# A gated attention and GLU kernel: where the splits of the row maxima, the casts and the low parts of q and k stand in VectorE's and ScalarE's order

## The chip, the core and the metric

The kernel runs on one core of a Trainium2 chip. The time is the device time of one execution in microseconds. The kernel before took 734.03 us (median of three runs, 732.46 to 734.10).

## The reference, cut to what matters

```python
def _A_ref(x, wqkv, wo):                      # S = 2048, D = 512, H = 32 heads of 16, window W = 256
    qkv = (x @ wqkv).reshape(B, S, 3, H, Dh).transpose(2, 0, 3, 1, 4)
    q, k, v = qkv[0], qkv[1], qkv[2]
    scores = einsum("bhqd,bhkd->bhqk", q, k) * Dh ** -0.5
    mask = (i - j >= 0) & (i - j < W)
    p = softmax(where(mask, scores, -1e9))
    return einsum("bhqk,bhkd->bhqd", p, v).transpose(0, 2, 1, 3).reshape(B, S, D) @ wo

def _B_ref(x, w_gate, w_up, w_down):          # F = 1376
    return (sigmoid(x @ w_gate) * (x @ w_up)) @ w_down

g = sigmoid((x * gate_w).sum(-1, keepdims=True))
return g * _A_ref(x, wqkv, wo) + (1 - g) * _B_ref(x, w_gate, w_up, w_down)
```

All is in fp32. The kernel makes each fp32 product out of three products of high and low parts (`mm3`): a high part is a cast to fp32r on ScalarE (ACT), a low part is the difference on VectorE (DVE).

## The kernel before

The order of the instructions on PE, ACT, DVE and SP (the queue of the DMAs) is the order in which the program writes them (`manual_schedule`). GpSimd (POOL) has only the masks here.

**Units.** The main loop `for u in range(N)` runs over units. A unit is a block of 128 queries in a group of four heads (8 groups of 16 blocks, 128 units). It has four steps, one for each head `hh`; a step is called a *slot* here. In a slot, PE makes the scores `s` (`s_part`, L370), from which DVE takes the row maximum (tile `mx`, L376), and the transposed scores `st` of nine units earlier (`st_part`, L425), of which ACT takes the exponential (L430). The two stand on different halves of the array and run side by side. Scores have two banks in turn (tag `s`, `bufs=2`): the `s` after next waits until DVE has read the maximum of this one.

**Fill.** Between them PE works on projections of q and k (`pj`), the gate and up products (`gu`) and later others, all through `group_mm` (L282), also two at a time on the two halves. `GAPS2` gives how many such pairs follow each slot: three in most, two in the *dense* slots. A *period* is eight units, 31 slots with a gap and one without.

**Bursts.** Every eighth unit (17, 25, ... 121, `visits[u] == 2`) starts with a long burst on PE: the products of probabilities and values for two blocks of 512 queries (`pv_part`, L460), the first into bank `pv`, the second into a bank with tag `st`. ACT copies each out (`o_take`, tile `ob`), and the transfers follow on SP. No slot runs meanwhile.

**Splits of the maxima.** Every fourth unit from 13 on (`mark`) `max_split` makes high and low parts of 16 columns of maxima, with three small DVE instructions (L386, L387, L391, tiles `nm` and `nt`), ahead of that unit's slots; `max_store` and `max_load` send them into the ring of operands. One of two such units is a burst's; the other is in the middle of the period (slot 16 of it).

**Guests.** Other small work is put into two lists, `acts` for ACT and `behind` for DVE, and taken from them in certain slots: the casts and low parts of weights (`w`, `wqh`, `wql`) and those of q and k. A q and k projection of one block is copied out of its bank by `proj_raw` (tile `pr`), cast by `proj_hi` (tile `sh`, L306), and its low part is made by `proj_lo` (tile `sl`, L310). Two of them make a stack, which goes to `stack_scratch` and comes back into the ring by `stack_load` (a fill and five loads, three DMAs a unit). Before, these casts and low parts were guests in the slots of the middle and of the end of a period.

**Masks.** `mask_p` issues one or two `affine_select` on POOL (L436, L442) at a unit's end, when its exponentials are made; so POOL works in the first one and a half slots of the next unit.

Of the kernel before, what the change touches and what calls it, by code (L numbers as in the profile page):

```python
# [39 lines left out]
LAG = 9  # L40
PVLAG = LAG + 4
# [3 lines left out]
QB = 32  # L45
HOLD = 3
GAPS = [3] * 12 + [2] * 3
GAPS2 = [3] * 8 + [2] * 3 + [3] * 6 + [2] * 3 + [3] * 8 + [2] * 3
SHIFT = 6
TURN = ((0, 2, 1), (1, 0, 2))  # L50
TAIL_LOAD = {109: 0, 110: 1, 114: 2, 115: 3}
# [14 lines left out]
def gated_mix_kernel(  # L66
# [53 lines left out]
    NP = NSTEP // 2  # L120
# [23 lines left out]
    with ExitStack() as actx:  # L144
# [466 lines left out]

        def proj_out(s):
            proj_raw(s)
            held.append((s, lambda: (proj_hi(s), behind.insert(0, lambda: proj_lo(s)))))

        halves = {}
        soon = []
# [115 lines left out]
        def flush(acts):  # L733
            while acts:
                acts.pop(0)()
# [89 lines left out]
        sdma = []  # L825
        wo_raw = []

        U_WIDE = NB * NWIDE + LAG
        visits = {u: 2 for u in range(PVLAG + 4, U_WIDE + 1, WIDE)}
        visits.update({u: 1 for u in range(U_WIDE + 4, N, 4)})  # L830

        proj_at = {5: [5], LAG: [6, 7], U_LAST: [NSTEP - 2], U_LAST + 1: [NSTEP - 1]}
        for s in range(8, NSTEP - 2):
            proj_at.setdefault(4 * s - (21 if s % 2 else 17), []).append(s)

        for u in range(N):
            if u == LAG:
                vctx.close()
                pctx = ExitStack()
                ppool = pctx.enter_context(tc.tile_pool(name="ppool", bufs=1))  # L840
                pbuf = ppool.tile([P, 15, HG, P], F32, name="pbuf")
                pv = ps.tile([P, CH], F32, tag="pv", name="pv", bufs=1)
            if u == 1:
                proj_post(NC)
            if u == 4:
                load_gu(0, 0)
                load_gu(0, 1)
            if u % 8 == 1 and u > 8 and u // 8 + 1 < NP:
                sdma = stack_load(u // 8 + 1)
            if u % 16 == 8 and u // 16 + 2 < NG:  # L850
                raw_q = load_wqk(u // 16 + 2)
            if u in (4, 8, NU):
                max_store(u // 4 - 1)
            mark = PVLAG <= u < NU and (u - PVLAG) % 4 == 0

            def transfers():
                if mark and visits.get(u) != 2:
                    run_dmas(later[:2])
                    del later[:2]
                    max_load((u - 5) // 4)  # L860
                run_dmas(later)
                later.clear()
                run_dmas(sdma[:SD])
                del sdma[:SD]

            if u in V_STORE:
                v_store(V_STORE[u])
            if not mark:
                transfers()
            if u in (5, LAG):  # L870
                max_load(u // 4 - 1)
            if u in V_LOAD:
                v_load(V_LOAD[u])
            if u in WD_LOAD:
                load_d(WD_LOAD[u])
            if u == NU:
                max_load(NSTEP - 1)
            if u in TAIL_LOAD:
                tail_load(TAIL_LOAD[u])
            if u == WO:  # L880
                both = apool.tile([P, ND, CH], F32, tag="w0", name="woraw")
                wo_raw.extend(both[:, d] for d in range(ND))
                nc.sync.dma_start(both, wo.rearrange("(c p) n -> p c n", p=P))
            for s4 in proj_at.get(u, ()):
                if u < LAG:
                    first.insert(0, (
                        lambda k, h, s4=s4: proj_slot(s4, k, h), lambda s4=s4: proj_sum(s4)))
                else:
                    work.append(proj_group(s4))
            while held and u >= 8 * (held[0][0] // 2) - 13:  # L890
                acts.append(held.pop(0)[1])
            if u == N - 1:
                hold_group(*rest.pop(0))
            for hh in range(HG):
                wide = visits.get(u) == 2
                if hh == 0 and u in visits:
                    s2 = (u - PVLAG) // 4 - wide
                    pv_part(s2, pv)
                if hh == 0 and mark:
                    max_split((u - 5) // 4)  # L900
                    run_dmas(later)
                    later.clear()
                    max_store((u - 5) // 4)
                if hh == 0 and wide:
                    flush(evac)
                    o_take(s2, pv)
                    run_dmas(later)
                    later.clear()
                    max_load((u - 5) // 4)
                    second = ps.tile([P, CH], F32, tag="st", name=f"pv{s2}", bufs=2)  # L910
                    pv_part(s2 + 1, second)
                    for guests, n in ((acts, 2), (behind, 4)):
                        for _ in range(min(n, len(guests))):
                            guests.pop(0)()
                    o_take(s2 + 1, second)
                elif hh == 0 and u in visits:
                    evac.append(lambda s2=s2: o_take(s2, pv))
                if hh == 2 and mark:
                    transfers()
                if u < NU:  # L920
                    s_part(u, hh)
                if 0 <= u - LAG < NU:
                    st_part(u - LAG, hh ^ 1 if u < NU else hh)
                if u < LAG:
                    flush(behind)
                    if hh % 2 == 1:
                        upto = n_first * (2 * u + 1 + hh // 2) // (2 * LAG)
                        run_first(upto - done)
                        done = upto
                else:  # L930
                    long = u < U_WIDE
                    k8 = (u - LAG) % WIDE * HG + hh
                    dense = GAPS2[max(0, k8 - 1)] < 3 if long else u < NU and (u - PVLAG) % 4 == 3 and hh > 0
                    k = (u - PVLAG) % 4 * HG + hh
                    at = k8 if long else k
                    guests, more = ((1, 3, 6, 12, 14, 21, 23, 26), (5, 25)) if long else ((1, 5, 9), (3, 7))
                    if behind and (u < PVLAG or u >= NU or at in guests or at in more and len(behind) > 2):
                        behind.pop(0)()
                    if evac:
                        evac.pop(0)()  # L940
                    elif acts and not dense and (u < NU or hh % 2 == 1):
                        acts.pop(0)()
                if u >= LAG and (hh % 2 == 1 or u < NU) and (u + 1 not in visits or hh < HG - 1):
                    if u < N - 2:
                        next(slots)
            if u < LAG:
                flush(soon)
            if u == LAG - 1:
                split_gu(0, 0)
                split_gu(0, 1)  # L950
            if u in (3, 7, NU - 1):
                max_split(u // 4)
            if u // 16 + 2 < NG:
                if u % 16 == 10:
                    acts.append(lambda g=u // 16 + 2, r=raw_q: (
                        split_wqk(g, r, 0), behind.insert(0, lambda: split_wqk(g, r, 1))))
            if 0 <= u - LAG < NU:
                mask_p(u - LAG)
            if u in TAIL_SPLIT:
                acts.append(lambda d=TAIL_SPLIT[u]: tail_split(d))  # L960
            if u in WD_SPLIT:
                acts.append(lambda f=WD_SPLIT[u]: split_d(f, True))
            if u in WO_SPLIT:
                acts.extend(lambda d=d: wo_split(d) for d in range(WO_SPLIT[u], WO_SPLIT[u] + 1))
            if u in SUMS:
                sums_load(SUMS[u])
            if u - 2 in SUMS:
                behind.append(lambda c=SUMS[u - 2]: later.append(sums_invert(c)))
            if u == TREAD:
                tail_reads(0)  # L970
            if u >= TREAD:
                tail_read(0, 2)
            for n in H_LOAD.get(u, ()):
                h_load(n)
            if u == N - 1:
                pctx.close()
                lpool = actx.enter_context(tc.tile_pool(name="lpool", bufs=1))
                gates = lpool.tile([P, 4 * NB], F32, name="gates")
                gs, omg = gates[:, 0:NB], gates[:, NB:2 * NB]
                spare = [lpool.tile([P, CH], F32, name=f"spare{k}") for k in range(6)]  # L980
            if u >= N - 2:
                flush(evac)
                flush(acts)
                flush(behind)
                h_skew(u - N - 1)
# [164 lines left out]
```

## Time and profile before

| | |
|---|---|
| median of three runs | 734.03 us (732.46 to 734.10) |
| the profiled execution | 733.71 us, its span 731.7 us |
| PE busy | 720.6 us of the span |
| PE weight loads busy | 591.8 us |
| DVE busy | 485.4 us |
| ACT busy | 427.5 us |
| POOL busy | 167.1 us |
| granted TensorE clock | 1.00 |

The span is what the profiler saw of the program; the execution's own time is 2.0 us more. Matmuls overlap, and their ends are modelled, so the pitch of the starts tells more than the busy time. A row of the timeline has the start in us, the duration in us, the engine, the line, the instruction, and in brackets how long the engine idled before it and what released it.

### The profile page before, as it was taken

What the parts mean: (1) busy time and instruction counts of PE and PEld (TensorE: products, weight loads), DVE (VectorE), ACT (ScalarE), POOL (GpSimd) and SP (SyncE); (2) the same over time, 40 slices, a digit from 0 to 9 for tenths busy, and PEclk for the clock granted to TensorE, in tenths of its full rate; (3) what the DMA queues carried; (4) which work ended last, traced back from release to release, by engine and by line L of the source; (5) the groups of instructions that cost most, each with busy time, mean ns of one, the idle gap of its engine ahead of it and who ended that gap; (6) DMA issues with size and microseconds to landing.
All of it is one profiled execution on the core that took longest, in us unless ns stands there. A gap on an engine that the chain in (4) does not pass through costs nothing.

```text
span 731.7 us, 17525 instructions
## 1 busy us (share of the span) xinstructions
PE 720.6 (98%) x6298; PEld 591.8 (81%) x6298; DVE 485.4 (66%) x1455; ACT 427.5 (58%) x890; POOL 167.1 (23%) x254
## 2 busy tenths in 40 slices
PE   9999999999999999999999999999999999999997
PEld 7888888878787787887878778798878888888886
DVE  5379857657585675867667586675837777658481
ACT  6423766667576676757758666675667664534341
POOL 5200323223242232323223332232332000000000
PEclk9999999999999999999999999999999999999999
DMA  8476644544464445635445445454577987879431
GB/s 297 113 203 201 211 147 182 164 158 169 125 229 155 152 130 170 213 118 198 149 148 181 154 156 181 166 173 131 177 227 196 252 239 184 217 174 252 127 80 57
DMA packets 104814, 127.22 MB, mean 174 GB/s; under 512 B 46718, under 2 KB 63614, under 8 KB 104728
## 3 DMA queue, kind: packets, MB, share of 16 engines
q1 hardware_dynamic: 104584, 125.98, 55.8%
q8 instruction: 49, 0.80, 0.5%
q14 instruction: 37, 0.30, 0.1%
q10 hardware_dynamic: 144, 0.13, 0.1%
HBM read 71.80 MB, written 51.13 MB: 168 GB/s over the span
## 4 chain that ended last, share of the span: by engine, by line
PE 89%; DVE 6%; issue 3%; DMA 1%; SPq 0%; ACT 0%; DVEq 0%
PE gu L282 22%; PE pv L460 11%; PE pj L282 11%; PE s L370 6%; PE tp L598 6%; PE st L425 5%; PE pd L94 5%; PE pd L96 5%; PE pd L95 5%; DVE junk L376 4%; PE vh L635 3%; PE pa L94 2%; PE pa L95 2%; PE pa L96 2%; PE vps L497 2%
## 5 line engine op out<-in xcount | busy, mean ns | idle before, releaser
L376 DVE CUSTOM_DVE_ANT_0 junk<-s,mask 128x384 f32<-128x384 f32 (+2 forms) x512 | 271.6, 530 | 136.0 <-PE s L370 71.9
L282 PE MATMUL gu<-xh,w 64*128 64x512 f32 x1152 | 272.2, 391 | 0.0
L282 PE MATMUL gu<-xl,w 64*128 64x512 f32 x576 | 184.7, 389 | 0.0
L370 PE MATMUL s<-ring 64*128 64x384 f32 (+2 forms) x536 | 167.2, 330 | 5.2 <-DVE mx L376 4.7
L430 ACT ACTIVATE pbuf<-st 128x384 f32<-128x384 f32 (+2 forms) x288 | 138.3, 491 | 57.3 <-PE st L425 31.5
L425 PE MATMUL st<-ring 64*128 64x384 f32 (+2 forms) x536 | 170.0, 334 | 0.9 <-DMA ring<-max_scratch 0.6
L282 PEld LDWEIGHTS gu<-xh,w 64*128 64x128 f32 x1152 | 155.7, 185 | 6.9
L430 ACT ACTIVATE V<-st 128x384 f32<-128x384 f32 (+2 forms) x224 | 101.3, 455 | 54.8 <-PE s L370 27.0
L370 PEld LDWEIGHTS s<-ring 64*128 64x128 f32 x536 | 95.0, 184 | 36.5 <-DVE mx L376 22.9
L436 POOL TENSOR_SCALAR_AFFINE_SELECT pbuf<-pbuf 128x512 f32<-128x512 f32 x72 | 46.8, 650 | 256.4 <-ACT pbuf L430 240.5
L425 PEld LDWEIGHTS st<-ring 64*128 64x128 f32 x536 | 95.5, 184 | 5.2 <-ACT V L430 1.6
L282 PEld LDWEIGHTS gu<-xl,w 64*128 64x128 f32 x576 | 90.8, 184 | 2.7
L282 PE MATMUL pj<-xh,wqh 64*128 64x512 f32 (+1 forms) x228 | 79.8, 391 | 0.0
L282 PE MATMUL pj<-xl,wqh 64*128 64x512 f32 (+1 forms) x228 | 79.5, 389 | 0.0
L282 PE MATMUL pj<-xh,wql 64*128 64x512 f32 (+1 forms) x228 | 69.6, 390 | 0.0
L436 POOL TENSOR_SCALAR_AFFINE_SELECT V<-V 128x512 f32<-128x512 f32 x56 | 36.8, 657 | 116.9 <-ACT V L430 112.2
L95 PE MATMUL pd<-ring,hb 128*128 128x512 f32 x160 | 62.3, 389 | 0.0
L96 PE MATMUL pd<-ring,hb 128*128 128x512 f32 x160 | 62.3, 389 | 0.0
L94 PE MATMUL pd<-ring,hb 128*128 128x512 f32 x160 | 62.3, 389 | 0.0
L90 ACT CAST hb<-V 128x512 fp32r<-128x512 f32 x40 | 24.9, 622 | 58.3 <-DVE V L798 44.8
L471 ACT COPY ob<-pv 128x512 f32<-128x512 f32 x32 | 18.8, 586 | 54.6 <-PE pv L460 51.5
L460 PE MATMUL pv<-pbuf,V 128*32 128x384 f32 (+2 forms) x848 | 49.5, 381 | 0.0
(131 smaller groups left out, 1280.2 us busy)
## 6 DMA issues: line engine op xcount, KB each, us to landing
gu_scratch<-sp SPq DMA_DIRECT2D x72, 256.0 KB
V<-gu_scratch SPq DMA_DIRECT2D x36, 512.0 KB
ring<-stack_scratch SPq DMA_DIRECT2D x56, 256.0 KB
stack_scratch<-sh SPq DMA_DIRECT2D x14, 512.0 KB
stack_scratch<-sl SPq DMA_DIRECT2D x14, 512.0 KB
ring<-stack_scratch SPq DMA_DIRECT2D x14, 512.0 KB
guraw<-in_wgu_dram SPq DMA_DIRECT2D x18, 256.0 KB
v_scratch<-V SPq DMA_DIRECT2D x4, 1088.0 KB
```

Source lines behind the costliest of these rows:

```text
L90: nc.scalar.copy(hi, src)
L94: mm(ps, lh, rh, start=first, stop=False)
L95: mm(ps, lh, rl, start=False, stop=False)
L96: mm(ps, ll, rh, start=False, stop=last)
L282: return mm(pt, (wl if w == 2 else wh)[r, d], (xl if w == 1 else xh)[r, d, c * CH:(c + 1) * CH], start=k == 0 and not second, stop=k == 3 ...
L370: mm(pt[:, (k - k0) * P:(e - k0) * P], lhsT, blk(g, k, hh, 1, e - k), start=k == k0, stop=e == i + 1, skip_group_check=True,)
L376: nc.vector.tensor_tensor_reduce(junk[:, 0:n], pt[:, 0:n], mask[:, 3 * P - n:], scale=1.0, scalar=NEG, op0=ALU.add, op1=ALU.max, accum_out ...
L425: mm(pt[:, (q - j) * P:(e - j) * P], lhsT, blk(g, q, hh, 0, e - q), start=q == j, stop=e == last, skip_group_check=True,)
L430: exps.append(nc.scalar.activation(p_blk(u, hh, 0, n), pt[:, 0:n * P].rearrange("p (b t) -> p b t", t=P), AF.Exp, scale=SCALE,))
L436: nc.gpsimd.affine_select(buf[:, s0], buf[:, s0], pattern=[[0, HG], [1, P]], compare_op=ALU.is_ge, fill=0.0, base=0, channel_multiplier=-1,)
L460: mm(bank[32 * hh:32 * hh + w, (q - q0) * P:(e - q0) * P], vt[:, v:v + w], p_blk(g * NB + j, hh, q - j, e - q), start=j == j0, stop=j == q ...
L598: return mm(tp[b][:, 0:TW], (xl if w == 1 else xh)[r, d, b * P:(b + 1) * P], tw[d][int(w == 2)][r, 0:TW], start=k == 0 and not second, sto ...
```

## The change

It has five parts.

1. `max_split` of a middle unit (`mid(u)`) is written one slot earlier, ahead of the last slot of the unit before.
2. The cast and low part of q and k leave the lists. `held` keeps the copies, and in the burst that comes before their stack is loaded, `proj_hi` of both stands ahead of the first `o_take`, `proj_lo` of both behind the transfers of the maxima; the stack's stores are issued there. Up to three more low parts are taken in the burst, four before.
3. Other low parts are taken in the long periods only at `hh == 2`, and not in the unit ahead of a middle unit.
4. The second group of dense slots goes from slots 17 to 19 to slots 21 to 23.
5. The projections of q and k are queued two units later, and `stack_load` starts one unit later, behind the burst.

```diff
-GAPS2 = [3] * 8 + [2] * 3 + [3] * 6 + [2] * 3 + [3] * 8 + [2] * 3
+GAPS2 = [3] * 8 + [2] * 3 + [3] * 10 + [2] * 3 + [3] * 4 + [2] * 3
...
         def proj_out(s):
             proj_raw(s)
-            held.append((s, lambda: (proj_hi(s), behind.insert(0, lambda: proj_lo(s)))))
+            held.append(s)
...
+        def mid(u):
+            return PVLAG <= u < NU and (u - PVLAG) % 4 == 0 and u not in visits
...
-            proj_at.setdefault(4 * s - (21 if s % 2 else 17), []).append(s)
+            proj_at.setdefault(4 * s - (19 if s % 2 else 15), []).append(s)
...
-            if u % 8 == 1 and u > 8 and u // 8 + 1 < NP:
+            if (u == LAG or u % 8 == 2 and u > 10) and u // 8 + 1 < NP:
                 sdma = stack_load(u // 8 + 1)
...
-            while held and u >= 8 * (held[0][0] // 2) - 13:
-                acts.append(held.pop(0)[1])
...
+                if hh == 3 and mid(u + 1):
+                    max_split((u - 4) // 4)
                 if hh == 0 and mark:
-                    max_split((u - 5) // 4)
+                    if not mid(u):
+                        max_split((u - 5) // 4)
                     run_dmas(later)
...
                 if hh == 0 and wide:
                     flush(evac)
+                    ripe = [held.pop(0) for _ in range(2) if held and held[0] // 2 == u // 8 + 1]
+                    for s4 in ripe:
+                        proj_hi(s4)
                     o_take(s2, pv)
                     run_dmas(later)
                     later.clear()
                     max_load((u - 5) // 4)
+                    for s4 in ripe:
+                        proj_lo(s4)
+                    run_dmas(later)
+                    later.clear()
                     second = ps.tile([P, CH], F32, tag="st", name=f"pv{s2}", bufs=2)
                     pv_part(s2 + 1, second)
-                    for guests, n in ((acts, 2), (behind, 4)):
+                    for guests, n in ((acts, 2), (behind, 3)):
...
-                    at = k8 if long else k
-                    guests, more = ((1, 3, 6, 12, 14, 21, 23, 26), (5, 25)) if long else ((1, 5, 9), (3, 7))
-                    if behind and (u < PVLAG or u >= NU or at in guests or at in more and len(behind) > 2):
+                    free = hh == 2 and not mid(u + 1) if long else k in (1, 5, 9) or k in (3, 7) and len(behind) > 2
+                    if behind and (u < PVLAG or u >= NU or free):
                         behind.pop(0)()
```

Three places show what moves. The first is DVE about the middle unit 61. `junk60_2` is the maximum of unit 60, head 2 (slot 14 of the period); `nm` and `nt` are the split; `sl18` is a low part of q and k. Before:

```order
L376 ISA junk60_2_4290,mx15_4254<-s60_2_4288,mask_153 128x384
L376 ISA mx15_4254 128x1
L310 TENSOR_TENSOR sl18_4264<-pr18_4244,sh18_4263 128x512
L376 ISA junk60_3_4304,mx15_4254<-s60_3_4302,mask_153 128x384
L376 ISA mx15_4254 128x1
L386 TENSOR_SCALAR nm14_4320<-mx14_3958 128x4x4
L387 SCALAR_TENSOR_TENSOR nm14_4320<-mx14_3958,nm14_4320 128x4x4
L391 STREAM_TRANSPOSE nt14_4323<-nm14_4320 128x32
L376 ISA junk61_0_4329,mx15_4254<-s61_0_4327,mask_153 128x384
L376 ISA mx15_4254 128x1
```

DVE at the same place now:

```order
L376 ISA junk60_2_4287,mx15_4255<-s60_2_4285,mask_153 128x384
L376 ISA mx15_4255 128x1
L386 TENSOR_SCALAR nm14_4298<-mx14_3950 128x4x4
L387 SCALAR_TENSOR_TENSOR nm14_4298<-mx14_3950,nm14_4298 128x4x4
L391 STREAM_TRANSPOSE nt14_4301<-nm14_4298 128x32
L376 ISA junk60_3_4305,mx15_4255<-s60_3_4303,mask_153 128x384
L376 ISA mx15_4255 128x1
L376 ISA junk61_0_4325,mx15_4255<-s61_0_4323,mask_153 128x384
L376 ISA mx15_4255 128x1
```

The low part is gone from there, and the split stands one slot earlier.

The second is ACT at the burst of unit 65 (`ob14` and `ob15` are the copies of the burst's two banks, `st63` and `st64` the scores of the slots on either side). Before:

```order
L430 ACTIVATE V_71<-st63_3_5059 128x128
L430 ACTIVATE V_71<-st63_2_5071 128x128
L471 COPY ob14_5105<-pv_869 128x512
L471 COPY ob15_5139<-pv14_5114 128x512
L430 ACTIVATE pbuf_868<-st64_1_5146 128x3x128
```

ACT at that burst now:

```order
L430 ACTIVATE V_71<-st63_3_5051 128x128
L430 ACTIVATE V_71<-st63_2_5063 128x128
L306 CAST sh20_5097<-pr20_4900 128x512
L306 CAST sh20_5097<-pr21_4930 128x512
L471 COPY ob14_5101<-pv_869 128x512
L471 COPY ob15_5139<-pv14_5114 128x512
L430 ACTIVATE pbuf_868<-st64_1_5146 128x3x128
```

Two casts stand ahead of the first copy. DVE has the two low parts in the same burst, behind that burst's split.

The third is SP behind the same burst. Before, the stores of this stack (`sh20`, `sl20`) were issued in the middle of the period ahead, and behind the burst stood the loads alone:

```order
L401 DMA ring_63<-max_scratch 4x16x32 x2
L344 DMA oT_scratch<-ob15_5139 16x512 x4
L344 DMA sum_scratch<-ob15_5139 4x512
L344 DMA ring_63<-fill_scratch 4x2x1024
L344 DMA ring_63<-stack_scratch 32x4x1024
```

SP there now:

```order
L401 DMA ring_63<-max_scratch 4x16x32 x2
L344 DMA stack_scratch<-sh20_5097 128x1024
L344 DMA stack_scratch<-sl20_5098 128x1024
L344 DMA oT_scratch<-ob15_5139 16x512 x4
L344 DMA sum_scratch<-ob15_5139 4x512
L344 DMA gu_scratch<-sp4_2_1_5182 128x512
L344 DMA ring_63<-fill_scratch 4x2x1024
L344 DMA ring_63<-stack_scratch 32x4x1024
```

The stores of a stack now stand between the burst and the loads of the same stack.

## The prediction

> **What bounds the kernel now.** I read the page first, for the engine that is full and the chain that ended last.
>
> ```profile
> PE 720.6 (98%) x6298; PEld 591.8 (81%) x6298; DVE 485.4 (66%) x1455; ACT 427.5 (58%) x890; POOL 167.1 (23%) x254
> ...
> PE 89%; DVE 6%; issue 3%; DMA 1%; SPq 0%; ACT 0%; DVEq 0%
> ```
>
> PE carries the chain, and DVE, two thirds busy, still has 6% of it. So there are places where PE waits for DVE. They are found by comparing the pitch of PE's starts with its own undisturbed pitch. The timeline of PE in the period from 188.22 gives that, with a short burst behind it; `s` is the start of a slot.
>
> ```profile
> 188.22 0.86 PE L460 MATMUL pv<-V 128*32 128x128 f32 x16
> 193.53 0.44 PE L370 MATMUL s<-ring 64*128 64x384 f32 x1
> 194.51 0.33 PE L370 MATMUL s<-ring 64*128 64x384 f32 x1
> 197.97 0.33 PE L370 MATMUL s<-ring 64*128 64x384 f32 x1
> 200.55 0.33 PE L370 MATMUL s<-ring 64*128 64x384 f32 x1
> 202.47 0.33 PE L370 MATMUL s<-ring 64*128 64x384 f32 x1
> 214.46 0.33 PE L370 MATMUL s<-ring 64*128 64x384 f32 x1
> 217.33 0.23 PE L370 MATMUL s<-ring 64*128 64x128 f32 x1
> 218.31 0.32 PE L370 MATMUL s<-ring 64*128 64x128 f32 x1
> 219.63 0.22 PE L370 MATMUL s<-ring 64*128 64x128 f32 x1
> 219.89 2.80 PE L460 MATMUL pv<-pbuf,V 128*32 128x384 f32 x48
> 224.56 0.38 PE L370 MATMUL s<-ring 64*128 64x256 f32 x1
> ```
>
> Slots 5, 6 and 7 (197.97 to 200.55) take 2.58 us: 0.86 with three pairs. Slots 8 to 10, the first dense group (to 202.47), take 1.92: 0.64 with two. Nothing is lost there. A period undisturbed is then 22 x 0.86 + 9 x 0.64 = 24.68, plus 0.26 for the slot without a gap (219.63 to 219.89), plus the burst: 5.31 for the long one (188.22 to 193.53), 4.67 for the short one (219.89 to 224.56). They alternate, so 30.25 and 29.61. The windows from burst to burst say what periods do take; second column is the length.
>
> ```profile
> 95.16:125.77 30.61, 30.14 (x321) 25.19 (x324) 20.91 (x73) 19.85 (x44) 9.19 (x15) 1.00 0.46 160
> 125.77:157.52 31.75, 31.42 (x344) 25.78 (x348) 21.35 (x77) 20.87 (x45) 9.66 (x15) 1.00 0.48 156
> ...
> 469.20:499.31 30.11, 29.81 (x321) 26.11 (x324) 20.01 (x73) 19.70 (x44) 9.31 (x15) 1.00 0.53 169
> sum 404.15, PE 398.44 PEld 325.45 DVE 273.12 ACT 265.25 POOL 123.42; mean PE 30.65 PEld 25.03 DVE 21.01 ACT 20.40 POOL 9.49
> ```
>
> Thirteen windows, seven with short bursts: 7 x 29.61 + 6 x 30.25 = 388.8 against 404.15. **The pool is 15.4 us**, 1.2 a period. Where it lies shows in the middle of a period, here of the one from 250.03 (PE first, then DVE, then POOL; the first DVE row is that of slot 5 above, undisturbed):
>
> ```profile
> 269.51 0.39 PE L370 MATMUL s<-ring 64*128 64x384 f32 x1
> 270.82 0.44 PE L370 MATMUL s<-ring 64*128 64x384 f32 x1 [0.46 <-DVE mx L376]
> 273.22 0.34 PE L370 MATMUL s<-ring 64*128 64x384 f32 x1
> ...
> 198.34 0.56 DVE L376 CUSTOM_DVE_ANT_0 junk<-s,mask 128x384 f32<-128x384 f32 x1 [0.30 <-PE st L425]
> ...
> 267.75 0.56 DVE L376 CUSTOM_DVE_ANT_0 junk<-s,mask 128x384 f32<-128x384 f32 x1
> 268.24 0.69 DVE L310 TENSOR_TENSOR sl<-pr,sh 128x512 fp32r<-128x512 f32 x1
> 268.84 0.56 DVE L376 CUSTOM_DVE_ANT_0 junk<-s,mask 128x384 f32<-128x384 f32 x1
> 269.52 0.55 DVE L387 SCALAR_TENSOR_TENSOR nm<-mx,nm 128x16 fp32r<-128x16 f32 x1
> 270.24 0.52 DVE L376 CUSTOM_DVE_ANT_0 junk<-s,mask 128x384 f32<-128x384 f32 x1
> 270.91 0.56 DVE L376 CUSTOM_DVE_ANT_0 junk<-s,mask 128x384 f32<-128x384 f32 x1
> 271.62 0.56 DVE L376 CUSTOM_DVE_ANT_0 junk<-s,mask 128x384 f32<-128x384 f32 x1
> ...
> 268.82 0.63 POOL L436 TENSOR_SCALAR_AFFINE_SELECT pbuf<-pbuf 128x512 f32<-128x512 f32 x1 [2.23 <-ACT pbuf L430]
> 269.41 0.63 POOL L442 TENSOR_SCALAR_AFFINE_SELECT pbuf<-pbuf 128x512 f32<-128x512 f32 x1
> ```
>
> From 269.51 to 273.22 stand slots 17 to 19 (dense) and 20: 3 x 0.64 + 0.86 = 2.78 by the pitch, 3.71 in fact. 0.93 is lost, 0.67 of it in the first of them, whose next `s` waits for DVE's `mx`. DVE had two things in a row: a low part, which put the maxima 1.09 apart (267.75 to 268.84), and the split, which put them 1.40 apart (to 270.24). Maxima alone come 0.71 apart (270.91 to 271.62). Within the split one instruction took 0.55, under POOL's two masks; without a mask it takes 0.17, as in a burst:
>
> ```profile
> 220.31 0.17 DVE L387 SCALAR_TENSOR_TENSOR nm<-mx,nm 128x16 fp32r<-128x16 f32 x1
> 213.81 1.12 DVE L544 TENSOR_TENSOR w<-guraw,w 128x512 fp32r<-128x512 f32 x1
> 213.75 0.64 POOL L436 TENSOR_SCALAR_AFFINE_SELECT V<-V 128x512 f32<-128x512 f32 x1 [2.09 <-ACT V L430]
> ```
>
> A low part too takes 1.12 when a mask has begun just before it, against 0.69 above. At the end of the period, slots 25 to 27 and dense 28 (214.46 to 218.31 in the first fence) took 3.85 for 3.22: 0.63 lost.
>
> **The ledger of a lag.** Take the lag to be how much later than usual a maximum starts. Usual is 0.37 behind its `s` (197.97 to 198.34). The `s` after next started 0.58 behind a maximum of 0.52 (270.24 to 270.82), so 0.62 behind one of 0.56: 1.0 together. So a lag costs nothing up to 2 x 0.86 - 1.0 = 0.72 among slots of three pairs, 0.86 + 0.64 - 1.0 = 0.50 where one of the two is dense, and 0.28 where both are. A slot of three pairs pays back 0.86 - 0.71 = 0.15; a dense slot adds 0.07. A low part without a mask adds 1.09 - 0.86 = 0.23, in a dense slot 1.09 - 0.64 = 0.45; a split under a mask 1.40 - 0.86 = 0.54; a split without one 0.38 less, 0.16.
>
> **The change, part by part.**
>
> *Split one slot earlier.* POOL's masks of 268.82 to 270.04 span from 0.69 ahead of slot 17 to 0.53 behind its start: the first slot and a half of a unit. Slot 14 is the third of its unit, so the split runs between two such stretches. So the split adds 0.16 to 0.23, on a lag which the first dense group left at 0.21 and four slots have paid back. Even with 0.54 it would stay below 0.72: 0.
>
> *Dense slots moved to 21 to 23.* The six slots of three pairs behind the split pay back up to 0.9. The group then begins from nothing, as the first does, which loses nothing.
>
> *Low parts of q and k in the burst.* Two for each of fourteen bursts. DVE and ACT are idle there:
>
> ```profile
> 222.11 0.59 ACT L471 COPY ob<-pv 128x512 f32<-128x512 f32 x1 [1.62 <-PE pv L460]
> 194.01 0.56 DVE L376 CUSTOM_DVE_ANT_0 junk<-s,mask 128x384 f32<-128x384 f32 x1 [4.19 <-PE st L425]
> ```
>
> DVE needs 2 x 0.69, with one or two more guests 2.8 of its 4.19: 0 on the path. ACT's two casts, at about the length of a copy, need 1.2 of 1.62. Where one more copy stands ahead, they come to 1.8, and the first `ob` may be 0.2 late; but its bank is needed only in the next burst. 0 as well. If this cover is gone, each burst grows by up to 1.2.
>
> *Low parts at `hh == 2`.* By the order, 17 guests are left in the first twelve periods, at slots 6, 10, 18, 22, 26 or 30 (the thirteenth has two of the tail's weights). With 0.23 or 0.45 and up to 0.21 of a dense group before them, those at 6, 10, 18, 26 and 30 stay within the bounds above. The two at 22 fall inside the dense group: 0.14 + 0.45 = 0.59 against 0.50. I take 0.1 each, between 0 and the 0.34 that the slot at 217.33 to 218.31 lost (0.98 for 0.64).
>
> *Projections and loads later.* A stack's two stores and its fill and five loads now follow one burst instead of being parted by half a period. What SP does and how long loads take:
>
> ```profile
> 195.33 1.84 SPq L344 DMA_DIRECT2D oT_scratch<-ob  x4
> 480.24 3.17 SPq L344 DMA_DIRECT2D ring<-stack_scratch  x5
> 483.46 5.27 DMA tailraw<-in_wgu_tail_dram
> ```
>
> The stores go out at 195.33, ahead of these transfers. Five loads (1.5 MB) and the 0.2 MB transfer behind them were down 8.5 us after the first issue (480.24 to 488.73). By that rate, as an estimate, the stores (1 MB) land within 8.5 us at worst and the loads 8.5 after: 212.3. The ring is first read at slot 28 (217.33): 5 us to spare, 0 on the path. On SP, what stands behind the waiting loads are stores of `sp`, whose five buffers now hold a q and k copy for up to a period; between none and the wait of one copy (0.59) in each period, I take 0, since a period has seven other copies, one in some 4 us, and a store of 0.25 MB is down before the third behind it, by the 8.5 us for 1.7 MB. The transfer at 483.46 held ACT in the last window. I leave 0.5 lost there, between 0 and as much again.
>
> **Sum.** Pool 15.4, less the first slot behind each burst, which stays (194.51 - 193.53 = 0.98 for 0.86: 13 x 0.1 = 1.3), less 0.2 for slot 22, less 0.5: 13.4. The period ahead of 95.16 has the same middle: 0.9 more, so 14.3 us. The profiled execution took 733.71 (span 731.7 and 2.0 around it), so 719.4; the median of 734.03 stands 0.3 above it: **719.7**.
>
> **Rivals.**
>
> *Half of it returns at the new place.* A guest at 18 or 22, or a copy waiting for a buffer, leaves a lag into the moved dense group, and 0.5 a period is lost again: 13 x 0.5 = 6.5, 726.2. For it: slots 25 to 28 lost 0.63 behind guests. Against: a low part under a mask (213.81) stood ahead of that, and only nine of the first twelve periods still have a guest behind slot 15.
>
> *PE is full anyway.* PE is busy 98%. If that busy time were work, only the idle time could be had, 731.7 - 720.6 = 11.1, and of the idle ahead of `s` only this:
>
> ```profile
> L370 PE MATMUL s<-ring 64*128 64x384 f32 (+2 forms) x536 | 167.2, 330 | 5.2 <-DVE mx L376 4.7
> ```
>
> That is 734.0 - 4.7 = 729.3. Against: of the 0.67 lost at 269.51 only 0.46 is shown idle, so busy time holds waiting. [...]
>
> *Slower: the ring comes late.* If stores and loads take 6 us longer than estimated, `s` waits 1 us at slot 28 in each of 13 periods: 733, the point from which it decides. At 7 us it is 746. For it: the chain from cast to store to load to score is now in one period, and the loads wait on SP for the stores' landing. Against: the estimate is itself the slow case.
>
> *Slower: GpSimd is held instead.* By row 213.81, DVE and POOL hold each other up. In the burst a low part could begin ahead of a mask that the second `pv` part reads, 0.69 each, two a burst: 14 x 1.4 = 19 us, 739. [...] Against: the split and the cast come first, so the mask begins first, and its block is read only in the last half microsecond of the burst.
>
> **How the numbers follow.** 0.70 for the forecast (between 717 and 724), 0.17 for half of it, 0.04 for PE full, 0.09 for the slower ones. The low end, 716.5, is the whole pool with twice the 0.9 ahead of it (734.0 - 17.2 = 716.8); the high end, 727.5, holds the half with 1.3 above it, and leaves the last three out. About 0.3% is what a measurement of this kernel can tell from no change: faster 0.90, same 0.03, slower 0.07.
>
> **What would show it.** Right: windows of 29.7 and 30.4 us from burst to burst; slots 17 to 20 at 0.86 and 21 to 23 at 0.64; `nm` L387 at 0.17 in every split; no more `s` waits for `mx` in the middle; bursts as long as now. Wrong: `s` at slot 28 released by a DMA, pitches of 0.7 and more in slots 21 to 24, `st` behind a burst waiting for `ob`, or POOL masks over 1 us in bursts.

## The result, and the profile after

The changed kernel takes 723.34 us (median of 4 runs, 722.29 to 723.47); the kernel before took 733.93 beside it (4 runs). The ratio is 0.9857, with a 95% interval of 0.9840 to 0.9874: 10.5 us faster. The forecast was 719.7, a gain of 14.3. The profiled execution took 723.27, at a granted clock of 1.00.

The page after, first its busy times and its chain:

```profile
PE 713.5 (99%) x6298; PEld 606.1 (84%) x6298; DVE 478.5 (66%) x1455; ACT 430.4 (60%) x890; POOL 165.6 (23%) x254
...
PE 98%; DMA 1%; issue 0%; DVE 0%; DVEq 0%
...
L425 PE MATMUL st<-ring 64*128 64x384 f32 (+2 forms) x536 | 166.6, 327 | 2.7 <-DMA ring<-max_scratch 2.5
L370 PE MATMUL s<-ring 64*128 64x384 f32 (+2 forms) x536 | 162.9, 322 | 0.0
```

DVE's 6% of the chain are gone, and `s` (L370) no longer stands idle: before it had 5.2 us ahead of it, most of it for `mx`. But `st` (L425) now stands idle 2.7, for a DMA.

The view of waits tells the same (total, times, longest). Before, of PE's weight loads:

```profile
PEld s L370 <- DVE mx L376: 22.9, 58, 1.1
```

After, of PE's weight loads:

```profile
PEld s L370 <- DVE mx L376: 2.1, 8, 0.4
PEld st L425 <- DMA ring<-max_scratch: 1.9, 2, 1.1
```

The middle of a period is now as the prediction drew it. After, in the period from 245.22 (PE's starts of `s`, then DVE, then POOL):

```profile
264.66 0.34 PE L370 MATMUL s<-ring 64*128 64x384 f32 x1
268.11 0.34 PE L370 MATMUL s<-ring 64*128 64x384 f32 x1
270.11 0.33 PE L370 MATMUL s<-ring 64*128 64x384 f32 x1
...
262.56 0.56 DVE L376 CUSTOM_DVE_ANT_0 junk<-s,mask 128x384 f32<-128x384 f32 x1
263.05 0.17 DVE L386 TENSOR_SCALAR nm<-mx 128x16 fp32r<-128x16 f32 x1
263.25 0.17 DVE L387 SCALAR_TENSOR_TENSOR nm<-mx,nm 128x16 fp32r<-128x16 f32 x1
263.59 0.52 DVE L376 CUSTOM_DVE_ANT_0 junk<-s,mask 128x384 f32<-128x384 f32 x1
...
261.15 0.63 POOL L442 TENSOR_SCALAR_AFFINE_SELECT pbuf<-pbuf 128x512 f32<-128x512 f32 x1
264.01 0.63 POOL L436 TENSOR_SCALAR_AFFINE_SELECT pbuf<-pbuf 128x512 f32<-128x512 f32 x1 [2.23 <-ACT pbuf L430]
```

The split lies between two stretches of masks, L387 takes 0.17 where it took 0.55, and the maxima on both sides of it start 1.03 apart (1.40 before). That is 0.17 over the pitch of 0.86, where the prediction had 0.16. Slots 17 to 20 (264.66 to 268.11) take 3.45, 0.86 each; the dense 21 to 23 (to 270.11) take 2.00 for 1.92. Nothing is lost to DVE.

The windows from burst to burst, after (second column is the length):

```profile
94.14:123.81 29.67, 29.67 (x318) 26.08 (x317) 20.77 (x73) 20.06 (x44) 9.64 (x15) 1.00 0.47 165
123.81:155.37 31.56, 31.19 (x342) 27.30 (x341) 20.76 (x77) 21.06 (x45) 9.20 (x15) 1.00 0.52 165
...
245.22:275.63 30.41, 30.41 (x330) 26.49 (x329) 21.43 (x78) 22.09 (x47) 9.18 (x15) 1.00 0.52 178
...
426.92:459.10 32.18, 30.83 (x329) 27.37 (x328) 20.57 (x77) 21.59 (x46) 9.19 (x15) 1.00 0.55 184
...
sum 394.64, PE 391.89 PEld 339.79 DVE 268.10 ACT 269.16 POOL 121.99; mean PE 30.15 PEld 26.14 DVE 20.62 ACT 20.70 POOL 9.38
```

The working forecast 404.15 - 13.4 = 390.75 for the sum; it is 394.64, 3.9 too much. The windows with short bursts are at or a little under what was worked out for them (29.4 to 29.7 for 29.71). The surplus is in those with long bursts, and not in all: 30.41 in one, 32.18 in another.

In five of those six, a wait stands at slot 24, right behind the moved dense group. From the chain after, in the window from 426.92:

```profile
451.41 1.87 DMA ring<-max_scratch
...
453.42 0.41 PE st L425
```

`st` waits there for the maxima of the middle split, which went to `max_scratch` and come back into the ring. What became late shows on SP. Before, in the window from 125.77:

```profile
146.15 0.32 SPq L394 DMA_DIRECT2D max_scratch<-nt  x1
147.64 1.18 SPq L401 DMA_DIRECT2D ring<-max_scratch  x2
```

After, in the window from 123.81:

```profile
139.71 2.05 SPq L344 DMA_DIRECT2D ring<-stack_scratch  x3
142.41 0.33 SPq L394 DMA_DIRECT2D max_scratch<-nt  x1
147.64 1.16 SPq L401 DMA_DIRECT2D ring<-max_scratch  x2
```

L394 is the store of the middle maxima, 16 KB; L401 is the load that waits for its landing. Before, 1.49 us lay between the two issues, and the stack's loads had been issued over 5 us earlier (136.63 to 140.92). Now the last of those loads go out just ahead of the store, and 5.23 us lie between. Over the thirteen middles it was about 1.5 in eight and 2.3 to 4.3 in the others before; now it is 2.1 to 5.7. The long window without a surplus, the one of 30.41, has 2.06. In all, SP waited there 27.1 us in 16 times before, and now:

```profile
SPq L401 <- DMA max_scratch<-nt: 55.5, 16, 5.0
```

The sign of this stood in the trace before. In its last window with a long burst the store (457.26) went out behind a stack's stores, its load followed 4.26 us later, and `st` waited at slot 24:

```profile
463.50 0.41 PE L425 MATMUL st<-ring 64*128 64x384 f32 x1 [0.60 <-DMA ring<-max_scratch]
```

Two readings come out of this, and they can both hold. One is the prediction's: the gain is VectorE's work taken out of the way. The other is new: the stack loads, moved behind the burst, hold up a small store behind them, and that eats 4 us of it. In the expectations A stands for the first and C for the second.

### The profile page after: what moved, and what is told of

Read it like the earlier page. It is cut to its first block, busy times and chain, and to the rows that moved or that the text cites. A ratio compares the mean times of both kernels' runs of the same rounds, so it can differ in the third digit from the quotient of the medians.

```text
span 721.4 us, 17549 instructions
## 1 busy us (share of the span) xinstructions
PE 713.5 (99%) x6298; PEld 606.1 (84%) x6298; DVE 478.5 (66%) x1455; ACT 430.4 (60%) x890; POOL 165.6 (23%) x254
## 4 chain that ended last, share of the span: by engine, by line
PE 98%; DMA 1%; issue 0%; DVE 0%; DVEq 0%
PE gu L282 28%; PE pj L282 12%; PE pv L460 11%; PE s L370 6%; PE st L425 6%; PE tp L598 6%; PE pd L96 5%; PE pd L95 5%; PE pd L94 5%; PE vh L635 3%; PE pa L94 2%; PE pa L95 2%; PE pa L96 2%; PE vps L497 2%; DMA ring<-max_scratch 1%; PE pd L1088 1%
## 5 line engine op out<-in xcount | busy, mean ns | idle before, releaser
L425 PE MATMUL st<-ring 64*128 64x384 f32 (+2 forms) x536 | 166.6, 327 | 2.7 <-DMA ring<-max_scratch 2.5
L370 PE MATMUL s<-ring 64*128 64x384 f32 (+2 forms) x536 | 162.9, 322 | 0.0
L370 PEld LDWEIGHTS s<-ring 64*128 64x128 f32 x536 | 95.2, 184 | 14.1 <-issue 3.0
L436 POOL TENSOR_SCALAR_AFFINE_SELECT pbuf<-pbuf 128x512 f32<-128x512 f32 x72 | 46.8, 651 | 253.2 <-ACT pbuf L430 239.1
L425 PEld LDWEIGHTS st<-ring 64*128 64x128 f32 x536 | 95.9, 184 | 7.7 <-DMA ring<-max_scratch 1.9
L442 POOL TENSOR_SCALAR_AFFINE_SELECT pbuf<-pbuf 128x512 f32<-128x512 f32 x70 | 44.9, 641 | 0.0
```

What stands on the lines that cost most here:

```text
L370: mm(pt[:, (k - k0) * P:(e - k0) * P], lhsT, blk(g, k, hh, 1, e - k), start=k == k0, stop=e == i + 1, skip_group_check=True,)
L425: mm(pt[:, (q - j) * P:(e - j) * P], lhsT, blk(g, q, hh, 0, e - q), start=q == j, stop=e == last, skip_group_check=True,)
L436: nc.gpsimd.affine_select(buf[:, s0], buf[:, s0], pattern=[[0, HG], [1, P]], compare_op=ALU.is_ge, fill=0.0, base=0, channel_multiplier=-1,)
L442: nc.gpsimd.affine_select(old, old, pattern=[[0, HG], [-1, P]], compare_op=ALU.is_gt, fill=0.0, base=0, channel_multiplier=1,)
```

## The experiments

All ratios are against the kernel before, run beside each.

**Dense slots alone.** The kernel before with the new `GAPS2`:

```diff
-GAPS2 = [3] * 8 + [2] * 3 + [3] * 6 + [2] * 3 + [3] * 8 + [2] * 3
+GAPS2 = [3] * 8 + [2] * 3 + [3] * 10 + [2] * 3 + [3] * 4 + [2] * 3
```

> The kernel before with the second dense group at slots 21 to 23 and nothing else. Theory A (a guest too many in a row in the middle is what costs, so each of the moves helps only as far as it parts them): the middle loses nothing any more (lag 0.23 + 0.54 = 0.77 against 0.72, paid back by slot 21), but the low part that the old order has at slot 21 now falls into the dense group and costs 0.3 to 0.5 in 11 of 13 periods: 727 to 731. Theory B (the place of the dense slots carries the gain by itself): about 13 x 0.9 less, 722 to 724.

Measured: 733.77, ratio 1.0009 (1.0000 to 1.0017). Nothing is won, and both expectations missed. DVE shows why. This kernel, around a split under masks with a low part ahead of it, then PE:

```profile
298.32 0.69 DVE L310 TENSOR_TENSOR sl<-pr,sh 128x512 fp32r<-128x512 f32 x1
298.92 0.55 DVE L376 CUSTOM_DVE_ANT_0 junk<-s,mask 128x384 f32<-128x384 f32 x1
299.40 0.59 DVE L386 TENSOR_SCALAR nm<-mx 128x16 fp32r<-128x16 f32 x1
300.02 0.55 DVE L387 SCALAR_TENSOR_TENSOR nm<-mx,nm 128x16 fp32r<-128x16 f32 x1
300.74 0.52 DVE L376 CUSTOM_DVE_ANT_0 junk<-s,mask 128x384 f32<-128x384 f32 x1
...
301.32 0.44 PE L370 MATMUL s<-ring 64*128 64x384 f32 x1 [0.24 <-DVE mx L376]
```

Here not one of the split's instructions was held but two, L386 (0.59) and L387 (0.55), and the maxima start 1.82 apart, not 1.40. With the low part's 0.23 that is past the bound of 0.72 even among slots of three pairs: 0.23 + 1.82 - 0.86 = 1.19. PE's `s` at 299.97, 301.32 and 302.30 show the loss: two slots take 2.33 for 1.72, so 0.6 is lost ahead of the dense group. The group then begins clean (0.63 and 0.63 for slots 21 and 22). But the old order has two low parts in it and right behind it, `w` L544 at 304.88 and `sl` L310 at 306.67, the second 0.90 long beside masks, and slots 23 to 26 take 3.72 for 3.22. That second loss of 0.5 is the one that Theory A expected; the first it put at nothing.

**Casts and low parts alone.** The kernel before with the parts on `held`, `ripe`, the projections and the loads, and with three low parts in the burst instead of four; the split, `GAPS2` and the rule for the other low parts stay as they were.

> The kernel before with the casts and low parts of q and k in the bursts and what that needs (later projections and loads); the split, the dense slots and the rule for the other guests as before. Theory A: the split under the masks alone leaves a lag of 0.54 into the dense group at 17, which costs 0.3 to 0.4 a period, and the late transfer of the maxima stays: 726 to 729. Theory B (the dense slots or the split's place carry the gain): 731 or more.

Measured: 729.68, ratio 0.9958 (0.9945 to 0.9972), 0.7 above A and below B. PE's weight loads still wait 14.8 us for `mx` (22.9 before).

**The change without the earlier split.**

```diff
-                if hh == 3 and mid(u + 1):
-                    max_split((u - 4) // 4)
                 if hh == 0 and mark:
-                    if not mid(u):
-                        max_split((u - 5) // 4)
+                    max_split((u - 5) // 4)
```

> The changed kernel with the split of the middle unit back at that unit's start, under GpSimd's masks. Theory A: a lag of 0.54 stays under 0.72 among slots of three pairs and is paid back before slot 21, so nothing is lost: 722.5 to 724.5, with the split's L387 at 0.5 us in each middle. Theory B: 13 x 0.4 to 0.5 comes back, 728 to 730.

Measured: 728.49, ratio 0.9933 (0.9910 to 0.9955). The time is B's, the reason is not: DVE lost nothing in the middle (2.9 us of waits for `mx` in all). But A's condition held only in part. L387 took 0.62 to 0.65 in five of the thirteen middles and 0.17 or 0.18 in the other eight, so most splits now escape the masks at the old place too. What grew are the waits for the maxima (10.2 us for PE and its weight loads, 4.4 in the change), since the store leaves a slot later, still behind the loads. SP of this kernel, in the period of the worst of them:

```profile
205.79 0.40 SPq L394 DMA_DIRECT2D max_scratch<-nt  x1
212.21 1.18 SPq L401 DMA_DIRECT2D ring<-max_scratch  x2
```

PE there:

```profile
214.22 0.65 PE L425 MATMUL st<-ring 64*128 64x384 f32 x1 [2.83 <-DMA ring<-max_scratch]
```

And the windows around it (the last three columns are the granted clock, the DMA share and GB/s):

```profile
186.00:211.00 25.00, 25.00 (x280) 21.24 (x277) 17.26 (x61) 16.59 (x36) 6.79 (x11) 1.00 0.55 173
211.00:214.00 3.00, 0.39 (x3) 0.02 (x1) 1.02 (x4) 0.28 (x1) 1.22 (x2) 0.89 0.03 7
214.00:217.00 3.00, 2.79 (x14) 2.82 (x16) 0.49 (x2) 1.43 (x3) 0.00 (x0) 0.50 0.68 223
217.00:220.00 3.00, 3.00 (x18) 3.00 (x17) 0.93 (x5) 0.78 (x3) 0.00 (x0) 0.50 0.15 56
```

A wait of 2.83 us was followed by some 6 us at half clock, with 14 to 18 matmul records in 3 us where 25 us before it hold 280. The four slots from the `s` at 211.06, the last ahead of the wait, took 9.28, where the same four of the run without loads, further down, took 3.45: the wait and the half clock together cost 5.83, about twice the wait's length.

**The change with the old `GAPS2`.** The line of the first experiment, the other way round.

> The changed kernel with the second dense group back at slots 17 to 19. Theory A: the split at slot 14 leaves a lag below 0.25, paid back by slot 17, so the group loses nothing but with the four guests at slot 18 (0.1 to 0.3 each): 723 to 725. Theory B: most of the 0.67 of a middle comes back, 729 to 732.

Measured: 725.46, ratio 0.9895 (0.9882 to 0.9908): 2.1 us over the change, just above A. DVE costs little here too (3.5 us of waits for `mx`); PE and its weight loads wait 7.5 us for the maxima, where they wait 4.4 with the change. So the 2.1 us are mostly a longer DMA wait, and once the split and the low parts are moved, little on DVE hangs on the place of the dense group.

**Part of the loads held back**, so that the store of the middle maxima has none just ahead of it:

```diff
-                run_dmas(sdma[:SD])
-                del sdma[:SD]
+                if u < PVLAG or u % 8 not in (3, 4):
+                    run_dmas(sdma[:SD])
+                    del sdma[:SD]
```

> The changed kernel with the second half of each stack's loads held back until the middle unit's maxima are stored and loaded. Theory C (the 16 KB store of the middle maxima stands behind the stack's loads and lands 5 us late, so st waits at slot 24 of every second period, 4.4 us in all): that wait goes, 718.5 to 720.5, with the store landing in about 1.5 us. If the loads held back come too late instead, s waits at slot 28 and it is over 724. Theory D (the landing is slow whatever stands ahead): 722.5 to 724.

Measured: 731.75, ratio 0.9984 (0.9975 to 0.9993). The waits at slot 24 are gone, but now the held back loads come too late for the score that reads the ring first. PE of this kernel:

```profile
123.05 0.29 PE L370 MATMUL s<-ring 64*128 64x128 f32 x1 [1.65 <-DMA ring<-stack_scratch]
```

Six such waits make 4.8 us, the longest 1.6. And a window just behind the one shown:

```profile
124.40:127.80 3.40, 3.40 (x32) 2.28 (x32) 2.52 (x10) 1.59 (x5) 0.63 (x1) 0.50 0.02 5
```

It runs at half clock (0.50). That is the rival "the ring comes late", brought about here; in the change itself no `s` waits for a DMA.

**The store on another queue.** The middle store is issued by ScalarE instead of SP:

```diff
-                    max_store((u - 5) // 4)
+                    max_store((u - 5) // 4, nc.scalar if mid(u) else nc.sync)
```

> The changed kernel with the 16 KB store of the middle maxima issued from ScalarE's queue instead of SyncE's. Theory C1 (what delays it is its place behind the loads in one queue): it lands in about 1.5 us and the wait at slot 24 goes, 718.5 to 720.5. Theory C2 (it is the DMA engines that are busy with the loads, whichever queue): 722.5 to 724, still landing late.

Measured: 721.95, ratio 0.9849 (0.9835 to 0.9862): between the two, and within the interval of the change (0.9840 to 0.9874). PE and its weight loads wait 2.2 us for the maxima, where they wait 4.4 in the change. The store still takes long. ScalarE's queue, then SP's, in this kernel:

```profile
142.68 0.33 ACTq L394 DMA_DIRECT2D max_scratch<-nt  x1
...
147.33 1.18 SPq L401 DMA_DIRECT2D ring<-max_scratch  x2
```

4.65 us for 5.23, so its place in SP's queue is at most a small part of the delay. The loads make the rest: with them left out of the change, further down, it is 1.45.

**All loads at once.** `SD = 6` instead of 3, all six transfers of a stack in one unit.

> The changed kernel with the fill and all five loads of a stack issued in one unit instead of two. Theory C: the last loads go out at most 1 to 2 us sooner, so the store still stands behind most of them and the wait at slot 24 shrinks but stays: 720.5 to 724. If only the issue of the store on SyncE is what is late, not the bytes ahead of it: 719 to 720.

Measured: 729.17, ratio 0.9943 (0.9930 to 0.9955). Missed: 5.8 us slower than the change. PE and its weight loads wait 6.6 us for the maxima, one wait 2.3 long. Between the store and its load lie 1.9 to 5.3 us over the thirteen middles, no more than in the change. So it isn't a slower store; what makes the waits longer stays open.

**No masks.** The kernel before with the two lines `if 0 <= u - LAG < NU:` and `mask_p(u - LAG)` taken out, so POOL's probability masks aren't computed; the rest is as before.

> The kernel before with GpSimd's masks of the probabilities left out (a part of the computation is missing, so only its time is read). Theory A (VectorE's guests cost because they run under the masks): the split's L387 falls from 0.55 to 0.18 and the low parts from up to 1.12 to 0.69, the middle loses at most 0.1 to 0.2 instead of 0.93: 720 to 725. Theory E (it is the number of guests in a row, masks or not): 730 or more.

Measured: 722.45, ratio 0.9856 (0.9843 to 0.9870), as A expects. With every guest at its old place, the masks alone make 10.4 us against the 732.89 of the kernel before beside it. PE's weight loads wait 7.7 us for `mx` there (22.9 before). The splits of this kernel between the first and the last burst, by groups:

```profile
L387 DVE SCALAR_TENSOR_TENSOR nm<-mx,nm 128x16 fp32r<-128x16 f32 x26 | 4.6, 175 | 0.9
L386 DVE TENSOR_SCALAR nm<-mx 128x16 fp32r<-128x16 f32 x26 | 4.4, 170 | 0.0
```

The low parts of q and k (L310) take 687 ns on average, 755 before. The splits before:

```profile
L387 DVE SCALAR_TENSOR_TENSOR nm<-mx,nm 128x16 fp32r<-128x16 f32 x26 | 9.2, 353 | 0.9
...
L386 DVE TENSOR_SCALAR nm<-mx 128x16 fp32r<-128x16 f32 x26 | 7.6, 290 | 0.0
```

After the change it is 4.6 us, 176 ns each: the change does for the splits what taking the masks away does. L386, of which the prediction showed no row, was held too before: 290 ns for 170.

**No loads.** The changed kernel with the five loads of each later stack left out (the scores then work on old data):

```diff
+            if t >= RING:
+                return dmas
```

> The changed kernel with the five loads of each later stack left out (the ring keeps older values, so only the time is read). Theory C (the loads ahead of it make the store of the middle maxima late): the store lands in 1.5 us, no st waits at slot 24, 718 to 719.5. Theory D (the landing is slow for another reason): 721.5 or more.

Measured: 719.62, ratio 0.9811 (0.9797 to 0.9825). The store and its load in the same period (L396 and L403 are L394 and L401, two lines lower):

```profile
143.29 0.32 SPq L396 DMA_DIRECT2D max_scratch<-nt  x1
144.74 1.13 SPq L403 DMA_DIRECT2D ring<-max_scratch  x2
```

1.45 us, as before the change, and no wait at slot 24 is left. Its last window with a long burst, and the sum of the thirteen:

```profile
425.15:455.82 30.67, 30.67 (x329) 25.20 (x329) 20.70 (x77) 21.52 (x46) 9.20 (x15) 1.00 0.43 141
sum 390.86, PE 390.82 PEld 334.72 DVE 268.17 ACT 269.11 POOL 122.17; mean PE 30.06 PEld 25.75 DVE 20.63 ACT 20.70 POOL 9.40
```

The window is 1.51 shorter than in the change, and the sum is 390.86 where the prediction had 390.75.

**Loads first.** A version that keeps every transfer but sends a stack's stores ahead of the burst's copies, and its loads right behind the burst's own maxima instead of over the next two units:

```diff
-            if (u == LAG or u % 8 == 2 and u > 10) and u // 8 + 1 < NP:
+            if u == LAG:
                 sdma = stack_load(u // 8 + 1)
...
                         proj_hi(s4)
+                    for s4 in ripe:
+                        proj_lo(s4)
+                    run_dmas(later)
+                    later.clear()
                     o_take(s2, pv)
                     run_dmas(later)
                     later.clear()
                     max_load((u - 5) // 4)
-                    for s4 in ripe:
-                        proj_lo(s4)
-                    run_dmas(later)
-                    later.clear()
+                    if u // 8 + 1 < NP:
+                        run_dmas(stack_load(u // 8 + 1))
```

> The changed kernel with a stack's stores issued ahead of the burst's first copies and its fill and loads ahead of the transfers of the burst's second copy, some 4 to 6 us sooner. Theory C: the loads are down before the store of the middle maxima goes out, the waits at slot 24 go, 718.5 to 720. If instead SyncE now holds up the copies' transfers, ScalarE's copies wait for buffers and it is 723 or more.

Measured: 720.63 (719.94 to 720.77), ratio 0.9824 (0.9811 to 0.9837), faster than both kernels. SP of this version, in the same period:

```profile
132.72 3.19 SPq L344 DMA_DIRECT2D ring<-stack_scratch  x5
...
143.30 0.32 SPq L394 DMA_DIRECT2D max_scratch<-nt  x1
144.91 1.18 SPq L401 DMA_DIRECT2D ring<-max_scratch  x2
```

The loads are out 7 us ahead of the store, whose load follows it after 1.61 (1.5 to 3.8 over the thirteen middles), and no wait at slot 24 is left. The sum of the thirteen windows is 391.63, 0.77 above the run without loads. All of it is in one window, the last with a long burst (31.50 for 30.67). There ACT, then PE, wait at slot 15:

```profile
443.38 0.59 ACT L558 COPY sp<-gu 128x512 f32<-128x512 f32 x1 [1.30 <-DMA oT_scratch<-ob]
...
444.02 0.50 PE L282 MATMUL gu<-xh,w 64*128 64x512 f32 x1 [0.55 <-ACT sp L558]
```

The tiles `sp` and `ob` take turns in the same five buffers (tag `sp`). The transfers of the burst's second copy now go out behind the loads, and the copy of `gu` waits for one of them to land: what the expectation named as the other outcome, in one place and small.

**Both.** That version with the middle store on ScalarE's queue as well.

> The one before, with the store of the middle maxima on ScalarE's queue as well. Theory C: nothing is left for the second queue to gain, within 0.1% of the one before, 718.5 to 720. Theory C1 (the queue): up to 1 us less.

Measured: 720.37 (720.01 to 720.72), ratio 0.9823 (0.9810 to 0.9836): the same. With the loads out of the way, the queue makes no difference that can be measured.

## Why the prediction was right, and where it was off

- **What was paid for.** Right: VectorE's small instructions under GpSimd's masks delayed `s`. Masks away, guests in place: 722.45. Guests away, masks in place: 723.34.
- **The pool and the first slot behind each burst.** Right in the mechanism; that the sum agrees so closely is partly luck. With the DMA wait taken away, the thirteen windows come to 390.86 for 390.75, and the gain to 13.7 us (719.62 against 733.34 beside it) for 14.3. But the seven windows with short bursts make 207.0 for the 208.5 worked out (7 x 29.71 and the 0.5 of the last), and the six with long ones 183.8 for 182.1 (6 x 30.35, slot 22 left out). The two errors, some 1.5 each, cancel. The longest, 31.14 and 30.82 (from 124.34 and from 304.72 in the run without loads), are two in which the first slots have their `s` in two matmuls; the working took its pitch from periods without these. The 0.2 for slot 22 and the 0.5 can't be seen apart.
- **Projections and loads later, 0 on the path.** This step failed. It asked whether the ring's own loads come in time for slot 28, and they do. It didn't ask what is sent behind them: the 16 KB of middle maxima, whose reader comes at slot 24. By the two ratios it cost 0.46% or 3.4 us, by the windows 394.64 - 390.86 = 3.8, about the whole miss (723.34 - 719.7 = 3.6). The order of SP behind the burst stood in the text; the next store on that queue, half a period later, was left out, though the trace before already had one such wait (463.50), which the working counted into the pool.
- **Split one slot earlier, 0.** Right on DVE, as the kernel without it showed (no loss at the old place, once the low parts are gone, though only five splits were under masks there). But the split also sets when the store leaves. With the loads ahead of it, a slot's delay cost 5.2 us here (728.49, single runs from 725.0 to 731.0), part of it the half clock. The step counted DVE alone.
- **The ledger.** Its 0.54 for a split under masks was the milder case. Before the change, L387 was held in twelve of the thirteen middles, and in six of these L386 was held too (0.54 to 0.62). There the maxima came 1.77 to 1.85 apart, so the split alone added 0.9 to 1.0. In the change no split runs there; the first experiment's expectation fell by it.
- **"Two things in a row".** In the period shown there were three. A low part of weights (`wql` L184, 266.11) took 1.03 beside a mask and put the maxima of slots 12 and 13 1.44 apart, ahead of the low part and the split. With it the ledger comes out: the maximum at 270.24 lagged by 270.24 - 268.70 - 0.37 = 1.17, which less the bound of 0.50 is the 0.67 lost. With the two alone it would be 0.23 + 0.54 - 0.50 = 0.27. By this working the rule for the other low parts, the third part of the change, has a share in the gain; no run tests it alone.
- **Casts and low parts in the bursts, 0.** Right: windows with short bursts are 29.4 to 29.7, against 29.71 worked out, and the bursts are as long as before (4.67 and 5.31).
- **The parts aren't a sum.** `GAPS2` alone wins nothing, the casts and loads alone 0.42%; without the moved dense slots the change loses 2.1 us, without the earlier split 5.2, in both cases for the most part by longer DMA waits.
- **The rivals.** *Half of it returns at the new place* is out: waits for `mx` fell from 22.9 to 2.1. *PE full* is out: 10.5 us were won where it allowed 4.7, and PE's busy share rose to 99% while the time fell. *GpSimd held* came in a small way and cost no time that can be seen: in five bursts of the change a mask took 1.08 (217.06; masks take 0.64 in the median) behind a low part of 0.70 that had begun 0.11 ahead of it (216.95). Before, the mask behind the low part of 213.81 took as long (1.08, at 214.34). That is some 0.45 in each of five bursts, where the rival had twice 0.69 in each of fourteen, and no burst grew (215.78 to 220.45 is 4.67). *The ring late* didn't happen, but a DMA wait of its kind did, for another transfer, and the held back loads showed how near it was.

## What to carry to other kernels

When a bulk transfer is moved, list the small transfers that are then issued behind it, and when each is read: the deadline that breaks is the neighbour's, not that of the moved data. Issue bulk loads where a gap in time follows them (720.63 us for 723.34 here, with the loads 7 us ahead of the small store); another queue hardly parted them here (4.65 us for 5.23). A 128x16 instruction took over three times its length beside GpSimd's masks (0.55 to 0.62 for 0.17), so its place can matter more than the number of them.

## What the runs showed of the hardware that was not expected

- In one and the same period, a 16 KB store let its load start 1.45 us after its own issue without the stack's loads (143.29 to 144.74), and 5.23 right behind them (142.41 to 147.64); from ScalarE's queue it was 4.65. Over the thirteen middles it was 1.45 to 3.2 without the loads and 2.1 to 5.7 behind them.
- PE's granted clock was 0.50 for 6 us (214 to 220) behind a wait of 2.83 us, in the kernel without the earlier split. In the kernel with loads held back it was also at 0.50 for 3.4 us, beginning 1.35 us after a wait of 1.65. Yet the kernel with all loads at once had a wait of 2.3, and that with the old `GAPS2` one of 2.1, and the mean clock of both was 1.000. So the length of a wait alone doesn't decide it; what else does, these runs don't show.
- Both 128x16 instructions of one split were held beside masks, in the kernel with the dense slots alone: L386 took 0.59 (299.40) and L387 0.55 (300.02), under two masks of 0.63 (299.33 and 299.91). With the masks left out they take 0.17 each (170 and 175 ns on average).
